# Sums z and dz off TensorE, mask by selects, and dWq blocks moved ahead of WK2, in a linear-attention block with its gradients

## The chip, the cores and the metric

The kernel runs on one core of one Trainium2 chip. The metric is device time in microseconds (us). The core has a TensorE (PE, matmuls), a VectorE (DVE), a ScalarE (ACT), a GpSimd (POOL) and a SyncE (SP, which mostly starts transfers). Every time below is the median of a kernel's executions, with the lowest and highest behind it. Ratios compare with executions of the kernel before on the same chip in the same session. A ratio is the mean time of one kernel's fast runs over the mean of the other's of the same rounds, so it is not quite the ratio of the medians quoted beside it. Its 95% interval stands in square brackets. A run counts as slow, and is left out of the ratio, when it is over 1.5% above the fastest of the same kernel.

## The reference, cut to what matters

The model is one block: a linear attention, then a gated MLP, each behind a layer norm, for 2048 tokens of width 640 (32 heads of 20). The program returns the output and the gradients of six of its inputs.

```python
def _A_ref(x, wqkv, wo):                     # H = 32, Dh = 20
    q, k, v = ...                            # x @ wqkv, split into heads
    phi = lambda t: jnp.where(t > 0, t + 1, jnp.exp(t)) + 1e-6
    pq, pk = phi(q), phi(k)
    kv  = jnp.einsum("bhsd,bhse->bhde", pk, v)
    z   = jnp.einsum("bhsd->bhd", pk)        # a sum over all tokens
    num = jnp.einsum("bhqd,bhde->bhqe", pq, kv)
    den = jnp.einsum("bhqd,bhd->bhq", pq, z)[..., None] + 1e-6
    return (num / den) ... @ wo
h   = x + _A_ref(_layernorm(x), wqkv, wo)
out = h + _B_ref(_layernorm(h), w_gate, w_up, w_down)
# returned: out and the vector-Jacobian product with grad_out
```

Two sums over the 2048 tokens (16 tiles of 128) matter here: z in the forward part, and dz, its gradient, in the backward part.

## The kernel before

TensorE makes both sums, as matmuls whose one operand is a block of ones (z) or the negative denominator terms nS (dz):

```python
# forward, behind the last projection
for ci, (n0, n1) in enumerate(NCH):          # two halves of 320 columns
    for t in range(ST):                      # 16 tiles of tokens
        nc.tensor.matmul(ps[q:q + H, ci, :320], lhsT=ones[:, :H], rhs=pk[:, t, n0:n1], ...)
...                                          # ScalarE and VectorE round z to two bf16 parts
def normalise(t):                            # VectorE, 4 tiles at a time, 4 times
    nc.vector.tensor_tensor(out=tz, in0=pq, in1=zb..., op=ALU.mult)          # needs z
    nc.vector.tensor_reduce(out=den[:], in_=hb4(tz), axis=AX.X, op=ALU.add)
    ...
    nc.vector.tensor_tensor(out=hb4(pq), in0=hb4(pq), in1=bc4(rall...), op=ALU.mult)
# pq is then transposed by SyncE's transfers, for the attention's output blocks ps_a
```

```python
# backward, stage of dhn and dp: one tile of 128 tokens at a time, the order of VectorE is the scheduler's
    pqr[u] = wk("pqr", pool=1)
    nc.gpsimd.dma_start(out=pqr[u][:], in_=scr_pq_v[:, u, :])        # GpSimd's queue
    nc.vector.tensor_tensor(out=hb(pqs_tm[:, u, :]), ...)            # phi(q), normalised: GT needs it
    ...
    # VectorE, "dp work" of tile u: pr, S1, nS1, pr, dp, pq, dp, dq
# after it: GT, then
dz_half(0); kv_blocks(dKVT, ...); dz_half(1)
...                                          # dz times E (one head's columns a row), x normalised
for i in range(DT): wk2(i)                   # WK2
...                                          # dzb: dz broadcast
dwqk(0, 0, 3)                                # three blocks of dWq, then the dK stage
```

The mask of the heads (ones in blocks) is made by two matmuls of E, a matrix built by GpSimd's selects.

The other names: xn is x normalised, Y its product with phi(k) summed over the tokens, KVT what Y becomes with the value weights, wvo the weights folded with KVT, ps_a the attention's output blocks. In the backward part dhn is the gradient behind the second layer norm (lb_ marks that norm's backward steps), cols its loaded operand, dp the gradient of the normalised phi(q), pqs_tm the normalised phi(q) itself, GT the product of dh and pqs_tm over the tokens. dWq is the gradient of the query weights, from dq and x normalised once more (hn); dKV and WK2 lead to dK. dwd is the gradient of w_down on its way out. A name with ps is a block in PSUM, where TensorE writes.

## Time and profile before

| | before |
|---|---|
| time, 3 runs | 821.57 us (821.45 to 823.08) |
| TensorE busy, at full clock | 813.3 of 820.0 us |
| first Y block / first ps_a / first dhn block start at | 57.2 / 100.1 / 456.0 us |
| last GT matmul / first dK matmul start at | 616.7 / 636.1 us |

The busy times, the chain at both places, and the slowed VectorE instructions stand in the prediction. Two further views matter later. The first gives, for stretches of time, the busy time of each engine, then the granted TensorE clock, the DMA share and the rate. It is the kernel before; the second line is the middle of the dhn stage.

```profile
core 0: us, PE busy (x) PEld busy (x) DVE busy (x) ACT busy (x) POOL busy (x), PEclk, DMA share, GB/s
87.50:106.00 18.50, 18.39 (x153) 11.39 (x151) 17.83 (x16) 9.32 (x12) 0.00 (x0) 1.00 0.58 136
517.00:578.00 61.00, 61.00 (x452) 43.94 (x450) 47.50 (x99) 17.48 (x28) 10.46 (x18) 1.00 0.69 189
```

VectorE is 54% busy on average, but 17.83 of 18.50 us just before and around the first ps_a block, where the normalising ends. In the dhn stage it has 13.5 of 61 us to spare.

### The profile page before, as it was taken

To read this page: it belongs to the slowest core of one execution; us is meant where nothing else is said; L and a number is where in the kernel's file an instruction comes from. 1 tells how busy PE (TensorE), PEld (TensorE's weight loads), DVE (VectorE), ACT (ScalarE), POOL (GpSimd) and SP (SyncE) were. 2 spreads that over 40 slices of the span, in tenths; PEclk is the share of its full clock that TensorE was granted. 3 is DMA by queue.
4 is the path that set the end of the run, shared out by engine and by line. 5 is a ranking of instruction groups with operands and counts; after the bars stand their busy time and mean duration, and the time that the engine had idled before them with its cause. 6 is when DMAs were issued, how large, how long until landed. Compare 5 with 4: busy or idle time off the path is not lost.

```text
span 820.0 us, 14053 instructions
## 1 busy us (share of the span) xinstructions
PE 813.3 (99%) x5540; PEld 521.0 (64%) x5540; DVE 442.9 (54%) x874; ACT 290.9 (35%) x412; POOL 187.6 (23%) x345
## 2 busy tenths in 40 slices
PE   8999999999999999999999999999999999999998
PEld 6776656555555555555566677777776777777675
DVE  6878776891087018810760147787884366631212
ACT  6982422770184126500741122322322133322010
POOL 3330022322412412221125311211210111112330
PEclk9999999999999999999999999999999999999999
DMA  9994589998769997894498757976498999899962
GB/s 297 186 343 113 140 174 281 307 204 176 191 126 209 203 224 160 185 245 115 106 237 171 256 139 217 222 205 166 116 216 171 170 167 187 167 198 272 222 176 76
DMA packets 278321, 158.61 MB, mean 193 GB/s; under 512 B 235052, under 2 KB 264877, under 8 KB 278256
## 3 DMA queue, kind: packets, MB, share of 16 engines
q1 hardware_dynamic: 251696, 82.12, 54.3%
q0 software_dynamic: 17744, 64.45, 25.8%
q10 hardware_dynamic: 8816, 11.16, 4.3%
q8 instruction: 43, 0.70, 0.4%
q14 instruction: 22, 0.18, 0.1%
HBM read 47.68 MB, written 53.66 MB: 124 GB/s over the span
## 4 chain that ended last, share of the span: by engine, by line
PE 82%; DVE 9%; ACT 3%; DMA 3%; issue 1%; SPq 1%; ACTq 0%; POOL 0%; DVEq 0%
PE ps_dw L627 21%; PE ps_dhn L109 14%; PE ps_dxn L877 8%; PE ps_o L937 7%; PE ps_dwqk L109 5%; PE pu L563 5%; PE pg L558 5%; PE ps_y L109 3%; PE ps_gt L678 3%; PE ps_dp L109 3%; PE ps_dk L109 3%; PE pdm L385 2%; DMA xr<-in_A_x_dram 2%; PE ps_dm L385 2%; DVE st L134 1%
## 5 line engine op out<-in xcount | busy, mean ns | idle before, releaser
L109 PE MATMUL ps_dhn<-wgT,cols 128*128 128x320 bf16 x864 | 119.5, 299 | 0.0
L627 PE MATMUL ps_dw<-dd,hn 128*128 128x448 bf16 (+1 forms) x640 | 118.8, 346 | 0.0
L109 PEld LDWEIGHTS <-cols 128*128 128x128 bf16 x864 | 84.5, 98 | 32.9
L627 PEld LDWEIGHTS <-hn 128*128 128x128 bf16 x640 | 62.6, 98 | 54.2
L629 DVE CAST dwev<-ps_dw 128x896 bf16<-128x896 f32 (+3 forms) x12 | 10.9, 907 | 122.9 <-PE ps_dw L627 122.9
L629 ACT CAST dwev<-ps_dw 128x896 bf16<-128x896 f32 (+1 forms) x20 | 17.6, 879 | 160.5 <-PE ps_dw L627 139.9
L592 POOL DMA_DIRECT2D scr_dT<-stg x64 | 34.7, 542 | 168.9 <-DMA stg<-dd 168.2
L147 DVE CUSTOM_DVE_ANT_0 lb_a<-lb_dy,hn 128x640 bf16<-128x640 bf16 x32 | 26.4, 825 | 75.4 <-ACT lb_dy L145 75.4
L563 PE MATMUL pu<-wgu,hnT 128*128 128x448 bf16 (+1 forms) x320 | 63.6, 346 | 0.0
L558 PE MATMUL pg<-wgu,hnT 128*128 128x448 bf16 (+1 forms) x320 | 63.6, 346 | 0.0
L937 PE MATMUL ps_o<-wd,mT 128*128 128x320 bf16 (+3 forms) x462 | 61.3, 295 | 0.0
L627 PE MATMUL ps_dw<-m_s,dh 128*128 128x448 bf16 (+1 forms) x320 | 60.5, 346 | 0.1
L877 PEld LDWEIGHTS <-ring 128*128 128x128 bf16 x480 | 47.0, 98 | 18.2
L937 PEld LDWEIGHTS <-mT 128*128 128x128 bf16 (+1 forms) x462 | 41.8, 97 | 17.6 <-issue 2.6
L877 PE MATMUL ps_dxn<-wqkvT,ring 128*128 128x320 bf16 x320 | 51.3, 299 | 0.0
L627 PEld LDWEIGHTS <-dh 128*128 128x128 bf16 x320 | 31.3, 98 | 27.4 <-issue 0.4
L563 PEld LDWEIGHTS <-hnT 128*128 128x128 bf16 x320 | 31.3, 98 | 27.1
L558 PEld LDWEIGHTS <-hnT 128*128 128x128 bf16 x320 | 31.3, 98 | 27.0
L298 PE MATMUL ps_kq<-wqk,xnT 128*128 128x320 bf16 x320 | 46.4, 299 | 1.0 <-ACT xnT L290 1.0
L385 PEld LDWEIGHTS <-dh2T 128*128 128x128 bf16 x320 | 31.1, 98 | 25.1 <-issue 0.2
L385 PE MATMUL ps_dm<-wdT,dh2T 128*128 128x448 bf16 (+1 forms) x240 | 46.9, 344 | 0.1
L145 ACT ACTIVATE lb_dy<-ps_dhn,rstd 128x640 bf16<-128x640 f32 x16 | 12.7, 793 | 85.5 <-PE ps_dhn L109 85.5
(162 smaller groups left out, 1277.1 us busy)
## 6 DMA issues: line engine op xcount, KB each, us to landing
scr_dT<-stg POOLq DMA_DIRECT2D x48, 224.0 KB, 3.3
cols<-scr_dT POOLq DMA_DIRECT2D x6, 1728.0 KB, 8.0
scr_m<-m_s POOLq DMA_DIRECT2D x12, 448.0 KB, 4.7
cols<-scr_dT ACTq DMA_DIRECT2D x2, 1728.0 KB, 9.5
out_dram<-dwev POOLq DMA_DIRECT2D x30, 112.0 KB, 3.4
scr_dT<-stg POOLq DMA_DIRECT2D x16, 192.0 KB, 2.6
scr_pk<-pk SPq DMA_DIRECT2D x4, 640.0 KB, 8.4
scr_pq<-pqa SPq DMA_DIRECT2D x4, 640.0 KB, 8.7
```

What stands on the lines that cost most here:

```text
L109: nc.tensor.matmul(ps[:, ci, :320], lhsT=lhs(k), rhs=rhs(k, *NCH[ci]), start=(start and k == 0), stop=(stop and k == n - 1))
L147: nc.vector.tensor_tensor_reduce(out=a[:], in0=dy[:], in1=xhat, scale=1.0, scalar=0.0, op0=ALU.mult, op1=ALU.add, accum_out=sums[:, 1:2])
L298: nc.tensor.matmul(ps[:, ci, :320], lhsT=xnT[:, t, k, :], rhs=wqk[:, k, w0 + n0:w0 + n1], start=(k == 0), stop=(k == DT - 1))
L385: nc.tensor.matmul(ps[:, c, :w], lhsT=dh2T[:, kt, (t + c) * P:(t + c + 1) * P], rhs=wdT[:, kt, o:o + w], start=(kt == 0), stop=(kt == DT - 1))
L558: nc.tensor.matmul(pg[:, c, :w], lhsT=hnT[:, kt, (t + c) * P:(t + c + 1) * P], rhs=wg[:, kt, 0:w], start=(kt == 0), stop=(kt == DT - 1))
L563: nc.tensor.matmul(pu[:, c, :w], lhsT=hnT[:, kt, (t + c) * P:(t + c + 1) * P], rhs=wg[:, kt, w:2 * w], start=(kt == 0), stop=(kt == DT - 1))
L592: nc.gpsimd.dma_start(out=scr_dT[t + c, :, KO[g]:KO[g] + GK[g], :], in_=stg[:, :GK[g], :])
L627: nc.tensor.matmul(ps[:, c, :w], lhsT=lhs(t), rhs=rhs(t), start=(t == 0), stop=(t == ST - 1))
L629: copy(out=ev[:, :len(parts), :w], in_=ps[:, :len(parts), :w])
L678: nc.tensor.matmul(ps[:, ci, :320], lhsT=dh1[:, t, i * P:(i + 1) * P], rhs=pqs_tm[:, t, n0:n1], start=(t == 0), stop=(t == ST - 1))
L877: nc.tensor.matmul(ps[:, ci, :320], lhsT=lhs[:, i, :], rhs=rhs[:, i, n0:n1], start=(k == 0 and i == 0), stop=(k == 2 and i == DT - 1))
L937: nc.tensor.matmul(po(t, ci), lhsT=mTs[t // 4][r, t % 4, j, :], rhs=wd[r, j, n0:n1], start=(t, ci) not in opened, stop=last)
```

## The change

Its intent is to take out of TensorE's stream all that others could do: z goes to GpSimd (6 tiles) and VectorE (10 tiles), dz to GpSimd, and the mask to GpSimd's selects. The waits between GT and dK are filled with dWq blocks, for which x is normalised earlier.

```diff
+    NZ = 6
+    def z_pool():                                   # GpSimd, behind its last power
+        zp = zf[:]                                  # 128 x 640, fp32
+        nc.gpsimd.tensor_tensor(out=zp, in0=pk[:, 0, :], in1=pk[:, 1, :], op=ALU.add)
+        for t in range(2, NZ):
+            nc.gpsimd.tensor_tensor(out=zp, in0=zp, in1=pk[:, t, :], op=ALU.add)
-        ps = mm("ps_z")                             # 32 matmuls, and the mask's 2
+        for n0, n1 in NCH:
+            zd = work.tile([P, 320], FP32, name="zd", tag="w")
+            nc.vector.tensor_reduce(out=zd[:], in_=pk[:, NZ:, n0:n1].rearrange("p t d -> p d t"), axis=AX.X, op=ALU.add)
+            nc.vector.tensor_tensor(out=zd[:], in0=zd[:], in1=zf[:, n0:n1], op=ALU.add)
+            ...                                     # rounded to two parts, zs and zl
         for i in range(DT):                         # Y blocks
-            if i == 0: mm_row(ps_z, ...)            # broadcast of z
+            if i == 1: mm_row(ps_zb, ...)
 ... the dhn stage, tile by tile
+        def dz_add(u):
+            for n0, n1 in NCH:
+                nc.gpsimd.tensor_tensor(out=hb(dst), in0=hb(pqs_tm[:, u, n0:n1]), in1=nS1[...], op=ALU.mult)
+                if u: nc.gpsimd.tensor_tensor(out=zf[:, n0:n1], in0=zf[:, n0:n1], in1=dst, op=ALU.add)
+            if u > 0: dz_add(u - 1)
 ... behind GT
-        dz_half(0); kv_blocks(dKVT, ...); dz_half(1)
-        ...                                         # E, x normalised
-        for i in range(DT): wk2(i)
-        dwqk(0, 0, 3)
+        ...                                         # x normalised
+        dwqk(0, 0)
+        kv_blocks(dKVT, ...)
+        dwqk(0, 1)
+        for i in range(3): wk2(i)
+        dwqk(0, 2)
+        for i in range(3, DT): wk2(i)
```

More of the change, by code (lines that the diff above doesn't have):

```diff
@@ L139, in ln_rstd @@
         eng.tensor_scalar(out=v[:, :nt], in0=mv[:, :nt, 1], scalar1=1e-5, scalar2=None, op0=ALU.add)
-        nc.gpsimd.tensor_tensor(out=rstd[:, t0:t0 + nt], in0=v[:, :nt], in1=nhalf[:, :nt], op=ALU.pow)
+        return nc.gpsimd.tensor_tensor(out=rstd[:, t0:t0 + nt], in0=v[:, :nt], in1=nhalf[:, :nt], op=ALU.pow)
     def ln_bwd(ps, xhat, rstd_col, resid, dst, pool):
@@ L233 @@
         nc.vector.memset(ones[:], 1.0)
-        E = const.tile([P, D], BF16, name="E")
-    ones32 = const.tile([P, P], BF16, name="ones32")
-    nc.vector.memset(ones32[:], 1.0 / H)
+        zf = const.tile([P, D], FP32, name="zf")
     zpad = const.tile([P, 4, 64], BF16, name="zpad")
@@ L253, with masks @@
     wo6 = wvo[:, 5:11]
+    def masks():
+        nc.gpsimd.memset(mask[:], 1.0)
+        for c0, n, p0 in ((0, 6, 0), (120, 2, 88)):
+            m = mask[:, c0:c0 + n * Dh]
+            for sign in (1, -1):
+                nc.gpsimd.affine_select(
+                    out=m, in_=m, pattern=[[-sign * Dh, n], [0, Dh]], compare_op=ALU.is_ge, fill=0.0,
+                    base=-p0 if sign > 0 else p0 + Dh - 1, channel_multiplier=sign)
     xn = big.tile([P, ST, D], BF16, name="xn", tag="B")
@@ L273, in ln1_rstd @@
     def ln1_rstd(t):
-        ln_rstd(mv1[:, t:t + 1, :], rstd1, t, 1)
+        return ln_rstd(mv1[:, t:t + 1, :], rstd1, t, 1)
     def ln1(t):
@@ L354 @@
                 ln1_stats(t + 2)
-                ln1_rstd(t + 2)
+                last_pow = ln1_rstd(t + 2).ins
             if t == 1:
@@ L363 @@
         kq_phi(ST - 1)
-        ps = mm("ps_z")
-        for ci, (n0, n1) in enumerate(NCH):
-            for t in range(ST):
-                q = t % 4 * H
-                nc.tensor.matmul(ps[q:q + H, ci, :320], lhsT=ones[:, :H], rhs=pk[:, t, n0:n1],
-                                 start=(t < 4), stop=(t >= ST - 4))
-        zs = [wk("zs"), wk("zl")]
-        nc.scalar.copy(out=half(zs[0][:]), in_=row(ps))
-        last_zs = nc.vector.tensor_tensor(out=half(zs[1][:]), in0=row(ps), in1=half(zs[0][:]), op=ALU.subtract).ins
-        ps_z = mm("ps_zb")
+    def z_pool():
[3 more added lines that the diff above has]
+            nc.gpsimd.tensor_tensor(out=zp, in0=zp, in1=pk[:, t, :], op=ALU.add)
+    with tc.manual_schedule(engines={EngineType.Pool}):
+        with tc.issue_after(last_pow):
+            z_pool()
+        masks()
     dm_t = {0: strips.tile([P, ST, GM], BF16, name="dm0", tag="S")}
@@ L408, in dm @@
             next(dms, None)
-    def masks():
-        tc.keep_in_program_order(nc.gpsimd.memset(E[:H, :], 1.0))
-        for sign in (1, -1):
-            tc.keep_in_program_order(nc.gpsimd.affine_select(
-                out=E[:H, :], in_=E[:H, :], pattern=[[sign, D]], compare_op=ALU.is_ge, fill=0.0,
-                base=0 if sign > 0 else Dh - 1, channel_multiplier=-sign * Dh))
-        for q in range(H, P, H):
-            nc.gpsimd.dma_start(out=E[q:q + H, :], in_=E[:H, :])
-        ps = mm("ps_mask")
-        pm = ps[:, 0, :160]
-        nc.tensor.matmul(pm[:, :120], lhsT=E[:H, 0:P], rhs=E[:H, 0:120], start=True, stop=True)
-        nc.tensor.matmul(pm[:, 120:], lhsT=E[:H, D - P:D], rhs=E[:H, 600:D], start=True, stop=True)
-        nc.scalar.copy(out=mask[:], in_=pm)
     pqsT = big.tile([P, DT, S], BF16, name="pqsT", tag="B")
@@ L459 @@
         KVT = yk[:, DT * D:].rearrange("p (j c) -> p j c", j=HG)
-        with tc.issue_after(last_zs):
-            nc.vector.memset(KVT, 0.0)
+        zs = [wk("zs"), wk("zl")]
+        for n0, n1 in NCH:
+            zd = work.tile([P, 320], FP32, name="zd", tag="w")
+            nc.vector.tensor_reduce(out=zd[:], in_=pk[:, NZ:, n0:n1].rearrange("p t d -> p d t"), axis=AX.X, op=ALU.add)
+            nc.vector.tensor_tensor(out=zd[:], in0=zd[:], in1=zf[:, n0:n1], op=ALU.add)
+            nc.vector.tensor_copy(out=zs[0][:, n0:n1], in_=zd[:])
+            nc.vector.tensor_tensor(out=zs[1][:, n0:n1], in0=zd[:], in1=zs[0][:, n0:n1], op=ALU.subtract)
+        nc.vector.memset(KVT, 0.0)
         for i in range(DT):
@@ L465 @@
             nc.scalar.copy(out=half(Yt[:, i, :]), in_=row(ps))
-            if i == 0:
-                mm_row(ps_z, lambda k: ones32[:], lambda k, n0, n1: zs[k][:, n0:n1], 2)
-                nc.scalar.copy(out=half(zb[:]), in_=row(ps_z))
-                masks()
             if 0 < i < 4:
                 dm(1)
+            if i == 1:
+                ps = mm("ps_zb")
+                mm_row(ps, lambda k: ones[:], lambda k, n0, n1: zs[k][:, n0:n1], 2)
+                nc.scalar.copy(out=half(zb[:]), in_=row(ps))
         dm(1)
@@ L679, in gt_part @@
                                      start=(t == 0), stop=(t == ST - 1))
+        def dz_add(u):
+            for n0, n1 in NCH:
+                dst = small.tile([P, 320], FP32, name="dzt", tag="stg", bufs=3, padded_shape=[P, 448])[:] if u else zf[:, n0:n1]
+                nc.gpsimd.tensor_tensor(out=hb(dst), in0=hb(pqs_tm[:, u, n0:n1]),
+                                        in1=nS1[:, u, n0 // Dh:n1 // Dh].unsqueeze(2).to_broadcast([P, 320 // Dh, Dh]),
+                                        op=ALU.mult)
+                if u:
+                    nc.gpsimd.tensor_tensor(out=zf[:, n0:n1], in0=zf[:, n0:n1], in1=dst, op=ALU.add)
         dq = [strips.tile([P, 8, D], BF16, name="dq", tag="S") for _ in range(2)]
@@ L717 @@
                     gt_part(gts[i], i, 0, ST - 3)
+            if u > 0:
+                dz_add(u - 1)
             pq = pqr.pop(u)
@@ L734 @@
             nc.vector.tensor_tensor(out=hb(dq[u // 8][:, u % 8, :]), in0=hb(dp[:]), in1=bc(rall[:, u, :]), op=ALU.mult)
+        dz_add(ST - 1)
     with tc.manual_schedule(engines={EngineType.SP, EngineType.DVE}):
@@ L776 @@
         Y = mat(2 * HG * P + HG * D, HG, D)
-        nc.gpsimd.dma_start(out=mat_v(scr_GT), in_=GT)
-        nc.vector.memset(dKVT, 0.0)
-        ps_dz = mm("ps_dz")
-        def dz_half(ci):
-            n0, n1 = NCH[ci]
-            for t in range(ST):
-                q = t % 4 * H
-                nc.tensor.matmul(ps_dz[q:q + H, ci, :320], lhsT=nS1[:, t, :], rhs=pqs_tm[:, t, n0:n1],
-                                 start=(t < 4), stop=(t >= ST - 4))
-        dz_half(0)
-        kv_blocks(dKVT, "ps_dkvt", lambda i, a, b: woT[:, i, a:b], lambda i, a, b: GT[:, i, a:b])
-        dz_half(1)
-        dzE = [wk("dzE"), wk("dzL")]
-        ps = ps_dz
-        nc.vector.tensor_tensor(out=half(dzE[0][:]), in0=row(ps), in1=half(E[:]), op=ALU.mult)
-        nc.vector.tensor_tensor(out=half(dzE[1][:]), in0=row(ps), in1=half(dzE[0][:]), op=ALU.subtract)
-        nc.vector.tensor_tensor(out=dzE[1][:], in0=dzE[1][:], in1=E[:], op=ALU.mult)
-        for t in range(ST):
-            nc.vector.tensor_scalar(out=xn_r[:, t, :], in0=xn_r[:, t, :], scalar1=mv1[:, t, 0:1],
-                                    scalar2=rstd1[:, t:t + 1], op0=ALU.subtract, op1=ALU.mult)
         wvk = strips.tile([P, 2, DT, D], BF16, name="wvk", tag="S")
@@ L802, with load_pqT @@
         WK2 = wvk[:, 1]
+        ring = strips.tile([P, 10, DT, P], BF16, name="ring", tag="S")
+        def load_pqT(v):
+            nc.sync.dma_start_transpose(out=ring[:, 4 + v % 3], in_=scr_pk[v * P:(v + 1) * P, :])
+            nc.sync.dma_start_transpose(out=ring[:, 7 + v % 3], in_=dq[v // 8][:, v % 8, :])
         def wk2(i):
@@ L808, in wk2, with dwqk @@
             nc.sync.dma_start_transpose(out=WV2[:, :, i * P:(i + 1) * P], in_=WK2[:, i, :])
-        for i in range(DT):
+        def dwqk(which, i):
+            ev = wk("dwqk", pool=i % 2)
+            ps = mm("ps_dwqk")
+            mm_row(ps, lambda t: xn_r[:, t, i * P:(i + 1) * P],
+                   lambda t, n0, n1: dq[t // 8][:, t % 8, n0:n1] if which == 0 else dk[:, t, n0:n1], ST)
+            nc.scalar.copy(out=half(ev[:]), in_=row(ps))
+            nc.gpsimd.dma_start(out=out_2[i * P:(i + 1) * P, which * D:(which + 1) * D], in_=ev[:])
@@ new lines @@
+        for v in range(3):
+            load_pqT(v)
+        nc.gpsimd.dma_start(out=mat_v(scr_GT), in_=GT)
+        nc.vector.memset(dKVT, 0.0)
+        for t in range(ST):
+            nc.vector.tensor_scalar(out=xn_r[:, t, :], in0=xn_r[:, t, :], scalar1=mv1[:, t, 0:1],
+                                    scalar2=rstd1[:, t:t + 1], op0=ALU.subtract, op1=ALU.mult)
+        dwqk(0, 0)
+        kv_blocks(dKVT, "ps_dkvt", lambda i, a, b: woT[:, i, a:b], lambda i, a, b: GT[:, i, a:b])
+        dzs = [wk("dzs"), wk("dzl")]
@@ L811 @@
+        nc.vector.tensor_copy(out=dzs[0][:], in_=zf[:])
+        nc.vector.tensor_tensor(out=dzs[1][:], in0=zf[:], in1=dzs[0][:], op=ALU.subtract)
+        dwqk(0, 1)
+        for i in range(3):
+            wk2(i)
+        dwqk(0, 2)
+        for i in range(3, DT):
             wk2(i)
         ps = mm("ps_dzb")
-        mm_row(ps, lambda k: ones[:], lambda k, n0, n1: dzE[k][:, n0:n1], 2)
+        mm_row(ps, lambda k: ones[:], lambda k, n0, n1: dzs[k][:, n0:n1], 2)
         nc.scalar.copy(out=half(dzb[:]), in_=row(ps))
-        def dwqk(which, i0=0, i1=DT):
-            for i in range(i0, i1):
-                ev = wk("dwqk", pool=i % 2)
-                ps = mm("ps_dwqk")
-                mm_row(ps, lambda t: xn_r[:, t, i * P:(i + 1) * P],
-                       lambda t, n0, n1: dq[t // 8][:, t % 8, n0:n1] if which == 0 else dk[:, t, n0:n1], ST)
-                nc.scalar.copy(out=half(ev[:]), in_=row(ps))
-                nc.gpsimd.dma_start(out=out_2[i * P:(i + 1) * P, which * D:(which + 1) * D], in_=ev[:])
@@ L825 @@
-        ring = strips.tile([P, 10, DT, P], BF16, name="ring", tag="S")
-        def load_pqT(v):
-            nc.sync.dma_start_transpose(out=ring[:, 4 + v % 3], in_=scr_pk[v * P:(v + 1) * P, :])
-            nc.sync.dma_start_transpose(out=ring[:, 7 + v % 3], in_=dq[v // 8][:, v % 8, :])
-        for v in range(3):
-            load_pqT(v)
-        dwqk(0, 0, 3)
         dk = big.tile([P, ST, D], BF16, name="dk", tag="B")
@@ L844 @@
             if t in (2, 3):
-                dwqk(0, t + 1, t + 2)
+                dwqk(0, t + 1)
             if t < ST:
@@ L870 @@
             if t >= ST:
-                dwqk(1, t - ST, t - ST + 1)
+                dwqk(1, t - ST)
             pkT, dqT, dkT = ring[:, 4 + u % 3], ring[:, 7 + u % 3], ring[:, u % 4]
@@ L890 @@
         nc.sync.dma_start(out=wd[64:, 13, :], in_=B_w_down[13 * P:F, :])
-        dwqk(1, LAG)
+        for i in range(LAG, DT):
+            dwqk(1, i)
         def dwo(j):
```

## The prediction

> **What bounds the kernel now.** I read the busy times first, then the chain of work that ended last, then the timelines around the two places where the sums z and dz are made, and last the groups of VectorE in the stage where dz would move to GpSimd.
>
> ```profile
> PE 813.3 (99%) x5540; PEld 521.0 (64%) x5540; DVE 442.9 (54%) x874; ACT 290.9 (35%) x412; POOL 187.6 (23%) x345
> ...
> PE 82%; DVE 9%; ACT 3%; DMA 3%; issue 1%; SPq 1%; ACTq 0%; POOL 0%; DVEq 0%
> ```
>
> TensorE is busy in 813.3 of 820.0 us at full clock. So this change can win only what it takes out of TensorE's stream, plus the small gaps at the same places; and it can lose whenever another engine makes TensorE wait. The chain (start, length, what) gives the pieces that the change touches:
>
> ```profile
> 56.45 0.84 PE ps_z L370 x17
> 57.29 4.45 PE ps_y L109 x32
> 61.74 0.54 PE ps_zb L109 x4
> 62.28 0.15 PE ps_mask L421
> 62.44 0.02 PE ps_mask L422
> ```
>
> ```profile
> 617.00 0.66 PE ps_dz L786 x16
> 617.66 1.54 PE ps_dkvt L484 x30
> 619.21 0.66 PE ps_dz L786 x16
> 619.86 0.43 PE ps_wk L128 x7
> 620.29 0.02 issue
> 620.31 1.30 ACT wvk L807 x2
> 621.61 0.04 issue
> 621.65 0.45 PE ps_wk L128 x7
> 622.10 0.64 PE ps_dzb L109 x4
> 622.75 13.52 PE ps_dwqk L109 x96
> ```
>
> The reader sees that z (32 matmuls) and dz (32) are already short, some 0.045 us a matmul, and that between 619.86 and 622.10 the chain leaves TensorE for ScalarE's evictions of WK2.
>
> The next lines decide how much is given back. They are from the timeline of all engines while phi(k), phi(q) of the last tokens are made, where GpSimd runs the two selects that build E:
>
> ```profile
> 50.41 1.49 POOL L414 TENSOR_SCALAR_AFFINE_SELECT E<-E 32x640 bf16<-32x640 bf16 x2
> 50.44 0.86 DVE L317 TENSOR_SCALAR phi_e<-phi_e 128x640 bf16<-128x640 bf16 x1
> ...
> 51.40 0.84 DVE L319 TENSOR_TENSOR pk<-phi_e,phi_r 128x640 bf16<-128x640 bf16 x1
> ...
> 52.16 0.31 DVE L317 TENSOR_SCALAR phi_e<-phi_e 128x640 bf16<-128x640 bf16 x1
> ...
> 52.58 0.49 DVE L319 TENSOR_TENSOR pqa<-phi_e,phi_r 128x640 bf16<-128x640 bf16 x1
> ```
>
> The same two VectorE instructions take 0.31 and 0.49 us when GpSimd is quiet and 0.86 and 0.84 us when a GpSimd select of 0.71 us runs beside them: 0.55 and 0.35 us longer, nearly what was left of the select at that moment.
>
> **What the Trainium skill says.** "SBUF — State Buffer", section "Who interferes with whom": VectorE and GpSimd share one pair of SBUF ports as an exclusive lock; a VectorE instruction with two SBUF inputs, or in a two-port mode, and a GpSimd instruction that reads SBUF shut each other out for a whole instruction; a reduction on VectorE does not contend. The trace agrees (0.86 against 0.31 us above). "GPSIMD Engine Reference", section "Elementwise — side-by-side cycle accounting": an add of two tensors costs GpSimd 4497 ns for 2048 elements a lane, some 2.6 cycles each. The trace has no wide GpSimd add; its selects with one input give 0.291 us for 128 and 0.708 us for 640 elements, so 0.19 us fixed and 0.81 ns an element. "VectorE: DVE Perf Modes", section "The perf-mode tier table": a reduction runs at one element a cycle. The trace agrees: 2560 elements in 2.82 us.
>
> **The change part by part.**
>
> Gains on TensorE. (1) z: its projections end at 55.55, the first Y block starts at 57.29. Without z the Y block can start at once, since the last pk tile is only its 16th operand: 1.74 us. (2) The mask matmuls: 0.17 us. (3) dz: 2 x 0.66 = 1.32 us. (4) WK2: five blocks of 7 matmuls; 21 of them took 1.06 us unhindered, so five take 1.77 us, against 622.10 - 619.86 = 2.24 us with the wait for evictions. Three and two, with a dWq block between, fit into the four PSUM buffers: 0.47 us. (5) dWq: 96 matmuls take 13.52 us; the 32 of a later block take 4.35, so three blocks need 13.04. The rest was TensorE pacing behind the normalising of x (16 x 0.36 us), which now starts before: 0.48 us. Sum 4.18 us, so the floor is 817.4 us. The dWq blocks themselves only move. The transposes that feed the last backward stage keep their number; load order changes, and WK2 is ready with room before the dxn blocks.
>
> Cost, z. VectorE reduces 10 of 16 tiles: 2 halves x 3200 elements at 2.82/2560 us is 3.5 us each, then an add, a cast and a subtraction of 320 columns, about 1.1 us: 9.2 us after the last phi at 57.6, so z is there at 66.8. The matmuls that broadcast it come after two Y blocks and one dm block: 55.55 + 4.35 + 4.35 + 1.89 = 66.15. TensorE would wait about 0.3 to 0.6 us; I take 0.3. The following normalisation starts 4 us later than now, but VectorE today waits 7.9 us for the KVT blocks, which covers that.
>
> GpSimd sums 6 tiles in 5 adds of 640 columns, right behind the last power at 49.76. From the select's rate and two reads an element an add is 0.19 + 640 x 2 x 0.81/1000 = 1.23 us; by the page's figure about 1.5 us. Estimates both. If each shuts VectorE out for its whole length less some 0.13 us (the 0.15 and 0.12 us by which the two cases above fall short), five add 5.5 us to VectorE. It had 0.2 us of idle time and 0.9 us of hindrance by the old selects there, so the xn tile of L270 at 55.12, which the Y block needs as its second operand, would come some 4.4 us late. Full effect on the start of Y: 4.4 us. I take 2.4 us, because VectorE's instructions come back to back there, may keep the ports, and GpSimd then does its adds in the free time later, up to 65 us.
>
> Cost, dz. Four GpSimd instructions of 320 columns a tile, 0.19 + 320 x 1.62/1000 = 0.71 us (0.88 by the page): 2.8 to 3.5 us a tile. VectorE's room there:
>
> ```profile
> 495.23 0.82 DVE L147 CUSTOM_DVE_ANT_0 lb_a<-lb_dy,hn 128x640 bf16<-128x640 bf16 x1 [1.67 <-ACT lb_dy L145]
> ...
> 496.86 0.82 DVE L727 TENSOR_REDUCE S<-pr 128x32 f32<-128x640 bf16 x1
> ```
>
> A tile takes 8.69 us of TensorE, and VectorE is idle in 1.7 of it. Shut out for 4 x (0.71 - 0.13) = 2.3 us, less one instruction (0.6 us) that falls beside the reduction, it loses 1.7 us a tile: just its idle time. At 0.88 us it is 2.3 us a tile, 0.6 us too much, and 15 tiles end 9 us late. The three tiles of lag hide that until the end, where GT, the normalising of x (611.9 + 5.8 = 617.7, needed in steps until 619.2) and the first dWq block then wait. I take 0.5 us. The dzb matmuls now come some 15 us after GT, so the last GpSimd sum is in time. GpSimd's own day, 3.2 us of work plus 1.6 us of DMA issue and waits in 8.69, leaves the column loads on time.
>
> Sum: 821.6 - 4.2 + 0.3 + 2.4 + 0.5 = 820.6 us.
>
> **The rivals.** A, the plain reading: GpSimd is idle there, its adds cost nothing. For it: 23% busy, 54% for VectorE, and someone chose 6 of 16 tiles so that z is just in time. Time 817.5 to 818.5. B, the port lock takes the place of the matmuls at the front: Y starts up to 3 us later than now, dz fits. Against A speaks the 0.86 us line. Time 821 to 823. C, as B, and VectorE becomes the bound of the stage of dhn and dp, because 7.0 us of its own and over 2 us of lock exceed 8.69 us: 826 to 835. For it: the page's GpSimd rate; against it: the room of three tiles, and that the lock falls partly on fixed overhead. D, GpSimd's loads behind dz_add come late (xnT_r waits now for the last dz): needed at 636, some 20 us after the queue is free; I see no cost.
>
> **Range and chances.** A gets about 0.4, B 0.35, C 0.2. The floor is 817.4, so faster by 2% (under 805.5) is all but excluded. Slower by 2% (over 838) needs C with GpSimd instructions of 1.1 us or more: 0.06. Eight in ten: 816.8 to 829.
>
> **What would show it.** In the changed profile: no group for z, dz and the mask on TensorE; TensorE's busy time some 3 us less; the first Y block starting at 55.6 (A), or at 58 to 60 (B) with phi and xn instructions of 1 to 1.8 us on VectorE beside GpSimd's adds; adds of 640 columns at 1.2 to 1.6 us and those of 320 at 0.7 to 0.9. In the dhn stage VectorE's two-input instructions get longer by some 2 us a tile and its waits for ScalarE's lb_dy shrink from 1.7 us; if that wait stays, C is wrong; if it is gone and GT or the first dWq block waits for VectorE, C is right. WK2 without a gap, and dWq blocks of 4.35 us. I would be wrong if GpSimd's adds leave VectorE's durations unchanged, or if they last over 2 us.

## The result, and the profile after

The changed kernel takes 846.04 us (841.93 to 849.68, 4 runs) against 822.33 (821.45 to 823.60, 4 runs) of the kernel before in the same session. The ratio is 1.0286 [1.0228, 1.0344]: slower, where the prediction gave that 0.06. The profiled execution, 849.68 us, is the slowest of the four; its numbers lean to the bad side.

From the page of the changed kernel, the busy times and the shares of the chain:

```profile
PE 820.0 (97%) x5474; PEld 524.1 (62%) x5474; DVE 493.2 (58%) x879; ACT 290.7 (34%) x410; POOL 252.5 (30%) x411
...
PE 77%; DVE 13%; DMA 6%; issue 2%; POOL 1%; SPq 1%; ACT 1%; DVEq 0%; POOLq 0%
```

TensorE runs 66 instructions less, as intended, and yet is busy 6.7 us longer, and the chain leaves it oftener. VectorE's busy time grew by 50 us, although z's reductions, additions and roundings are only 2 x (5.62 + 0.49 + 0.32 + 0.49) = 13.8 us of work. What TensorE waited for (total us, times, longest):

```profile
PE ps_gt L675 <- DVE pqs_tm L707: 7.0, 2, 4.7
PE ps_dhn L110 <- DMA cols<-scr_dT: 5.6, 1, 5.6
PE ps_y L110 <- DVE xn L278: 3.8, 2, 2.1
PE ps_a L110 <- DMA wvo<-wvo: 2.2, 2, 1.6
PE ps_zb L110 <- DVE zs L456: 1.6, 1, 1.6
```

Before, no wait of TensorE except those for the first tiles was above 0.3 us. The waits fall into two groups: the first Y block and what follows it, and the stage of dhn with GT. The first group in the timeline, GpSimd's sums beside VectorE:

```profile
49.33 0.49 DVE L327 TENSOR_TENSOR pqa<-phi_e,phi_r 128x640 bf16<-128x640 bf16 x1
49.38 1.69 POOL L375 TENSOR_TENSOR zf<-pk 128x640 f32<-128x640 bf16 x1
49.73 1.52 DVE L278 TENSOR_SCALAR xn<-x_tm,mv,rstd 128x640 bf16<-128x640 bf16 x1
...
51.15 5.95 POOL L377 TENSOR_TENSOR zf<-zf,pk 128x640 f32<-128x640 f32 x4
51.17 1.55 DVE L325 TENSOR_SCALAR phi_e<-phi_e 128x640 bf16<-128x640 bf16 x1
...
52.83 1.53 DVE L327 TENSOR_TENSOR pk<-phi_e,phi_r 128x640 bf16<-128x640 bf16 x1
```

Each of VectorE's instructions of 0.3 to 0.5 us waits one add through and ends soon after it; the lock is as the prediction has it. The same stretch by windows shows a term that the prediction lacks, in the column before the last two:

```profile
58.00:60.00 2.00, 0.35 (x1) 0.00 (x1) 1.79 (x6) 1.91 (x4) 0.83 (x3) 0.50 0.96 334
60.00:62.00 2.00, 1.91 (x8) 1.11 (x9) 1.86 (x4) 0.22 (x1) 0.00 (x0) 0.50 0.13 44
62.00:64.00 2.00, 2.00 (x9) 1.15 (x8) 2.00 (x1) 0.00 (x0) 0.00 (x0) 0.50 0.90 306
```

From 55.8 to 60.1 us TensorE did almost nothing (0.49 us of work). Its granted clock fell to 0.50 at 57.9, after 2.1 us of standing still, and came back at 64.7: 9 matmuls fit into 2 us there, against 17 in the 2 us from 66. The Trainium skill describes this in "TensorE: Matmul & The Clock Gate", section "What's actually happening": after an idle window of some 3.4 us the clock falls to half. I had not looked at that page. The half clock is in this trace (single matmuls of up to 474 ns, against 299), but not one length of idle time before it: 2.1 us here, 4.2 us at the wait for cols (idle from 582.7, half clock from 586.9). The profile has four such stretches, 23.9 us in all, in which TensorE was busy for some 19 us. If that work takes half the time at full clock, they cost some 9.5 us (an estimate). That is more than the matmuls taken away, and explains why TensorE is "busier" after the change.

Where the 28.0 us between the two profiles' spans (820.0 and 848.0) arose, by the start of the first matmul of each group:

| stretch | before | after | difference |
|---|---|---|---|
| start to first Y matmul | 57.2 | 57.9 | +0.7 |
| first Y matmul to first dhn matmul | 398.8 | 407.0 | +8.2 |
| first dhn matmul to last GT matmul | 160.7 | 182.2 | +21.5 |
| last GT matmul to first dK matmul | 19.4 | 16.7 | -2.7 |
| first dK matmul to the end | 183.9 | 184.2 | +0.3 |

The gain of 2.7 us is what was planned there: 2.27 us were predicted for dz, WK2 and the pacing of dWq. The five waits shown above (20.2 us) and the estimate for the half clock (9.5) make 29.7 us, near to the 28.0 us plus the 3 us of matmuls that TensorE no longer runs.

### The profile page after: what moved, and what is told of

Same layout as the page of the kernel before. It is cut to its first block, busy times and chain, and to the rows that moved or that the text cites. A ratio compares the mean times of both kernels' runs of the same rounds, so it can differ in the third digit from the quotient of the medians.

```text
span 848.0 us, 13992 instructions
## 1 busy us (share of the span) xinstructions
PE 820.0 (97%) x5474; PEld 524.1 (62%) x5474; DVE 493.2 (58%) x879; ACT 290.7 (34%) x410; POOL 252.5 (30%) x411
## 4 chain that ended last, share of the span: by engine, by line
PE 77%; DVE 13%; DMA 6%; issue 2%; POOL 1%; SPq 1%; ACT 1%; DVEq 0%; POOLq 0%
PE ps_dw L624 21%; PE ps_dxn L874 8%; PE ps_o L935 7%; PE pg L555 7%; PE pu L560 7%; PE ps_dhn L110 6%; PE ps_dwqk L110 5%; PE ps_dm L391 5%; DMA dwd<-scr_dwdT 3%; PE ps_dk L110 3%; PE ps_a L110 3%; PE pdm L391 2%; PE ps_y L110 2%; DVE st L135 1%; DVE zd L454 1%
## 5 line engine op out<-in xcount | busy, mean ns | idle before, releaser
L110 PE MATMUL ps_dhn<-wgT,cols 128*128 128x320 bf16 x864 | 122.1, 303 | 5.6 <-DMA cols<-scr_dT 5.6
L152 ACT ACTIVATE lb_a<-hn,lb_k 128x640 bf16<-128x640 bf16 x32 | 29.5, 921 | 49.5 <-DVE lb_k L151 35.3
```

The source lines that it names most:

```text
L110: nc.tensor.matmul(ps[:, ci, :320], lhsT=lhs(k), rhs=rhs(k, *NCH[ci]), start=(start and k == 0), stop=(stop and k == n - 1))
L152: nc.scalar.activation(out=a[:], in_=xhat, func=ACT.Identity, scale=k[:, 1:2], bias=k[:, 0:1])
```

## The experiments

Sixteen kernels ran, in four sessions. My first theory was the lock: GpSimd's sums hold the ports that VectorE needs, VectorE falls behind, and TensorE waits. The rivals were that the sums fill GpSimd's queue and make its loads late, that VectorE's own added work (the reductions) is the cost, and later, that only the order of VectorE's instructions changed.

### One half at a time

**Both sums back on TensorE**, with the selects, the early normalising of x and the new order kept:

```diff
-        with tc.issue_after(last_pow): z_pool()
+        ps = mm("ps_z"); ...                        # 32 matmuls as before
-            if u > 0: dz_add(u - 1)
+        ps_dz = mm("ps_dz"); ...                    # 32 matmuls behind GT, times E
```

> Both sums back on TensorE; the selects for the mask, the order of the dWq blocks and the early normalising of x stay. If the whole loss comes from the two sums: no TensorE wait over 1 us outside start and tail, clock 1.00 throughout, and 820 to 821 us, that is 0.95 us (WK2 0.47, dWq 0.48) plus 0.17 us (mask matmuls) below before. If the order of the dWq blocks or the late transposes carry part of the loss: above 823 us.

It took 822.13 us (821.87 to 823.84), ratio 1.0006 [0.9994, 1.0019]. The whole loss is in the two sums. The gain hoped for did not show: the first Y matmul started at 58.6 us here, against 57.2, and from there to the end the trace is 1.2 us shorter.

**Only z back on TensorE** (dz stays on GpSimd):

> z back on TensorE, dz left on GpSimd. Changed kernel: the first dhn matmul starts at 465 us against 456 before (9 us of the loss), and dhn to the end of GT takes 182 us against 161 (21 us). If the two losses are independent: dhn starts at 456 and the run takes about 21 - 2 us more than before, 838 to 843 us. If the late start feeds the second loss: less than 835 us.

833.46 us (832.98 to 834.71), ratio 1.0144 [1.0129, 1.0160].

**Only dz back on TensorE** (z stays on GpSimd and VectorE):

> dz back on TensorE, z left on GpSimd and VectorE. If independent: dhn starts at 465, dhn to the end of GT takes 161 us again, and the run takes about 9 - 1 us more than before, 828 to 831 us. If dz alone isn't what lengthens the dhn stage, that stage stays over 170 us.

831.96 us (831.38 to 834.82), ratio 1.0129 [1.0114, 1.0144].

So dz alone costs 1.44% and z alone 1.29%; their sum, 2.73%, is within the interval of the full change (1.0228 to 1.0344). By my criterion for the second run, under 835 would have meant that the late start feeds the second loss. The sum says otherwise: the halves add up. I had drawn the criterion from the one profiled execution, the slowest of four.

### What the lock holds

**GpSimd fills instead of sums**, of about the same length, in the full change; wrong:

```diff
-        nc.gpsimd.tensor_tensor(out=zp, in0=zp, in1=pk[:, t, :], op=ALU.add)
+        nc.gpsimd.memset(zp.bitcast(BF16), 1.0)     # and likewise in dz_add
```

> Wrong result on purpose: each GpSimd add and multiply of the two sums becomes a GpSimd fill of about the same length that reads nothing from SBUF (896 and 1280 two-byte elements, 0.8 and 1.1 us by the rate of the fills seen). GpSimd's queue stays as full. If the shared ports are the cause (theory L): VectorE's two-input instructions keep 0.49 and 0.82 us, dhn to the end of GT returns to 161 to 163 us, the first Y block starts before 57 us, and what is left is the late z of VectorE's reductions: 822 to 828 us in all. If GpSimd's full queue, which also issues the loads, is the cause (theory Q): the dhn stage stays at 175 us or more with the wait for the cols load.

851.89 us (849.29 to 853.67), ratio 1.0362, no better at all. My expectation fell, and the groups of VectorE in the dhn stage say why:

```profile
L730 DVE TENSOR_TENSOR pr<-dp,pqr 128x640 bf16<-128x640 bf16 x12 | 20.6, 1720 | 0.1
L151 DVE TENSOR_SCALAR lb_k<-lb_s 128x2 f32<-128x2 f32 x15 | 20.1, 1338 | 0.5
...
L153 DVE TENSOR_TENSOR lb_a<-lb_a,lb_dy 128x640 bf16<-128x640 bf16 x15 | 7.3, 489 | 4.1 <-ACT lb_a L152 4.0
L154 DVE TENSOR_TENSOR dh<-lb_a,dh 128x640 bf16<-128x640 bf16 x15 | 7.3, 484 | 0.1
```

The layer norm's instructions with two inputs (the last two lines) are as fast as in the kernel before (483 and 484 ns), as "SBUF — State Buffer", section "Who interferes with whom", has it for a GpSimd that only writes. But an instruction on 128x2 elements with one input takes 1338 ns on average, against 219. One of them took 5.96 us, through three transfer issues on GpSimd and four fills of 0.86 to 1.18 us. Of the instructions with two inputs only pr is longer (1720 ns, against 492): at the four places that were read in the timeline it starts just behind such an instruction and ends with it. The longest is another instruction with one input, near the end of the stage:

```profile
606.00 16.12 DVE L737 TENSOR_SCALAR pqr<-pqr 128x640 bf16<-128x640 bf16 x1
```

It lasted through fifteen fills and two transfer issues. The dh of the last tile stands behind it, and TensorE waited 17.0 us for dh1T, which is made from dh. A fill is no neutral stand-in for a sum.

**Powers instead of sums** for dz, on the kernel with z on TensorE; six powers of 128x1 a tile touch almost no memory; wrong:

```diff
-                nc.gpsimd.tensor_tensor(out=hb(dst), ..., op=ALU.mult)
-                if u: nc.gpsimd.tensor_tensor(out=zf[:, n0:n1], ..., op=ALU.add)
+                for k in range(3):
+                    nc.gpsimd.tensor_tensor(out=zf[:, n0 + k:n0 + k + 1], in0=rstd2[:, u:u + 1], in1=nhalf[:, :1], op=ALU.pow)
```

> Wrong result on purpose. z on TensorE; the four GpSimd instructions of dz a tile become six powers of 128x1, about 0.65 us each and so about as long (3.9 us a tile), which read and write one column. The powers seen in the first stage do not lengthen VectorE's instructions. Theory L (the SBUF ports): VectorE undisturbed, dhn to the end of GT 161 us as before instead of 174, time 821 to 823 us. Theory Q (GpSimd's queue too full to issue its loads in time): the stage stays at 170 us or more, time over 830 us.

823.24 us (821.93 to 824.32), ratio 1.0007 [0.9991, 1.0022]. The windows of 61 us in the middle of the dhn stage are the sharpest comparison. First with the dz sums, then with the powers, engines in the order PE, PEld, DVE, ACT, POOL:

```profile
518.00:579.00 61.00, 61.00 (x451) 43.93 (x449) 59.80 (x96) 17.49 (x28) 36.65 (x48) 1.00 0.84 199
```

```profile
519.00:580.00 61.00, 61.00 (x451) 43.94 (x450) 47.27 (x99) 17.48 (x28) 37.48 (x63) 1.00 0.66 197
```

GpSimd is as busy in both (36.65 and 37.48 us). VectorE does the same work; it takes 59.80 us beside the sums and 47.27 beside the powers, and 47.50 in the kernel before. A tile takes 8.69 us, so the lock costs VectorE 12.3 / 7.02 = 1.75 us a tile, of the 1.9 us that were idle. VectorE has 1.2 of 61 us left, and TensorE does not wait yet. GpSimd being busy is not the cause; what it touches is.

**dz for every second tile only** (the result passes the tolerance though half of dz is missing):

```diff
-            if u > 0:
+            if u > 0 and u % 2 == 1:
                 dz_add(u - 1)
```

> Wrong result on purpose. z on TensorE; dz on GpSimd for every second tile only. Theory L with VectorE's idle time of 1.7 us a tile as the threshold: a tile with dz costs VectorE about 2.4 us, so over two tiles 2.4 us against 3.4 us of idle time: no lag, dhn to the end of GT 161 to 163 us, time 821 to 824 us. If the loss is proportional to the number of GpSimd instructions, with no threshold: half of the 13 us, 827 to 829 us.

828.24 us median, but 824.01, 827.44 and 829.03 in the fast runs and 838.67 in one that counts as slow; ratio 1.0056 [1.0032, 1.0080]. In the profiled, fastest one TensorE waits 3.1 us for the last pqs_tm. With half the sums VectorE has room on average, and the time depends on how the last tiles fall. The ratio lies between the two theories and settles neither.

### The front: lock, stride, or neither

**The reductions of z with adjacent elements**, on the kernel with dz on TensorE; z is wrong on purpose, but passes the tolerance:

```diff
-  in_=pk[:, NZ:, n0:n1].rearrange("p t d -> p d t")                        # step of 640 elements
+  in_=pk[:, NZ:, n0:n1].rearrange("p t (a b) -> p t a b", b=10)            # adjacent
```

> Wrong result on purpose. dz on TensorE, z on GpSimd and VectorE as in the run that took 832.0 us; but VectorE's two reductions of 3200 elements read along the row (groups of 10 neighbours) and not with a step of 640 elements. If the step is what makes one reduction take 5.6 us and not the 3.5 us of the prediction: 3.5 us each, z ready 4.2 us earlier, TensorE's waits for z gone, and the first dhn matmul at 461 to 463 us instead of 466. If the length comes from something else: 5.6 us again and no change.

830.65 us (829.71 to 831.16), ratio 1.0101 [1.0087, 1.0115]. The reductions, first with the step and then without it (min/median/max in ns):

```profile
L464 DVE TENSOR_REDUCE zd<-pk x2: 5611/5615/5619, 62.2 to 69.5; 128x320 f32<-128x3200 bf16 x2
```

```profile
L464 DVE TENSOR_REDUCE zd<-pk x2: 3479/3482/3486, 62.3 to 67.5; 128x320 f32<-128x3200 bf16 x2
```

The prediction's 3.5 us is right for adjacent elements, from which its rate came; the change steps over 640 elements, and pays 1.61 times as much. TensorE's wait for zs is gone, but the first dhn matmul comes at 464.7 us, later than the 461 to 463 expected.

**No GpSimd sums of z** (one fill and ten powers in their place, the reductions as in the change), then **the same with adjacent elements**; z wrong in both:

```diff
-        nc.gpsimd.tensor_tensor(out=zp, in0=pk[:, 0, :], in1=pk[:, 1, :], op=ALU.add)   # and four more
+        nc.gpsimd.memset(zp, 1.0)
+        for k in range(10):
+            nc.gpsimd.tensor_tensor(out=zf[:, k:k + 1], in0=rstd1[:, ST - 1:ST], in1=nhalf[:, :1], op=ALU.pow)
```

> Base: the changed kernel with dz back on TensorE (831.96 us alone, ratio 1.0129). Here the five GpSimd adds of z are replaced by one fill and ten powers of 128x1, so nothing that shares memory ports with VectorE runs on GpSimd while x is normalised and the last feature maps are made; VectorE's two reductions, its additions and its roundings stay. z is wrong on purpose. Port theory of the front (the adds stretch VectorE's instructions from 0.3-0.5 to 1.5 us, which stops TensorE in the first Y and halves its clock): the first Y has no wait for xn (4.0 us before) and no matmul at half clock, and the time falls by 4 to 7 us to 825-828 (ratio about 1.0045-1.008). Chain theory (the two reductions of 5.6 us and what follows them on VectorE set the stage's end, whatever the adds do): the wait for xn goes, but the wait for zs and the late ps_a grow by as much, and the time stays above 830.

> As the run before, and the two reductions of VectorE read adjacent elements (3.48 us each as measured, 5.61 with a step of 640). z is wrong on purpose. If lock and slow reductions are the two parts of z's loss and add up: 822-825 (ratio 1.001-1.004), since 2 us more are saved than in the run before. If a third part exists (the reductions' mere presence on VectorE between the last feature map and the normalisation, some 10 us), it stays above 826.

826.36 us (826.08 to 828.24), ratio 1.0050 [1.0021, 1.0079], and 824.22 us (822.15 to 825.78), ratio 1.0018 [0.9988, 1.0048]. The waits of TensorE: the kernel with z's lock and step, then without the lock, then without both.

```profile
PE ps_y L110 <- DVE xn L279: 4.0, 2, 2.1
PE ps_a L110 <- DMA wvo<-wvo: 2.4, 2, 1.7
PE ps_zb L110 <- DVE zs L466: 2.2, 1, 2.2
```

```profile
PE ps_zb L110 <- DVE zs L466: 3.8, 1, 3.8
...
PE ps_a L110 <- DMA wvo<-wvo: 0.5, 1, 0.5
```

```profile
PE ps_a L110 <- DMA wvo<-wvo: 3.4, 2, 1.9
```

Without the lock the wait for xn is gone, and part of it comes back as a wait for zs, the end of the slow reductions. Without both, TensorE still waits 3.4 us before the attention's blocks. The order of these four traces, by the start of the first dhn matmul (456.0 in the kernel before):

| | lock | no lock |
|---|---|---|
| step of 640 | 466.4 | 461.7 |
| adjacent | 464.7 | 457.5 |

The lock is worth 4.7 or 7.2 us, the step 1.7 or 4.2, together 8.9; these are single executions, and the last is the fastest of its four. By the ratios of all runs the lock is worth 0.79 or 0.83% and the step 0.28 or 0.32%.

In the best corner nothing is gained, although TensorE has no z matmuls and starts its Y blocks at 55.7 us. It is through the last block ahead of ps_a at 98.9 us, against 100.3 in the kernel before, so most of the 1.74 us was still there. Then it waits for the transposes of wvo, as the last view says, and the first ps_a matmul comes at 100.3 us, against 100.1. VectorE's normalising is not late: its third part starts at 87.9 us, against 89.3. SyncE's transposes of wvo last from 92.2 to 101.8 us, against 92.5 to 99.5. In its queue they stand behind transfers that came some 5 us later than before (the transposes of pqsT at 84.9, against 79.9). That this slows them is not shown; why they were late stays open, and with it whether the 1.74 us could be had.

### The stage of dhn: loads and order

**cols from ScalarE's queue**, in the full change. In the profile of the changed kernel GpSimd's queue stood 8.61 us at a wait for dwd, and the load of cols behind it came late:

```profile
574.84 0.55 POOL L711 DMA_DIRECT2D out_dram<-dwd  x1 [8.61 <-DMA dwd<-scr_dwdT]
...
580.16 0.75 POOL L162 DMA_DIRECT2D cols<-scr_dT  x1
...
588.35 2.05 PE L110 MATMUL ps_dhn<-wgT,cols 128*128 128x320 bf16 x7 [5.61 <-DMA cols<-scr_dT]
```

```diff
-                    load_cols(t // 2 + 1)
+                    load_cols(t // 2 + 1, act_load)
```

> The changed kernel in full, with only the loads of cols issued from ScalarE's queue instead of GpSimd's, where they stood behind a wait of 8.6 us for dwd. If TensorE's wait of 5.6 us for cols (and the half clock after it, some 2 us more) is a loss of its own: 838-841 against 846. If it is only where a lag of VectorE shows first (the same lag would be waited for at GT): 844-848, with the wait for pqs_tm at GT grown from 7.0 to 10 us or more.

844.62 us (842.32 to 846.70), ratio 1.0276 [1.0241, 1.0310]. The wait for cols is gone from its profile, the wait for pqs_tm at GT is 7.6 us, neither smaller nor the 10 us of the second theory. The times do not separate it from the full change. Late cols may be part of why the profiled execution was the slowest of four; how often they come late in others stays open.

**Order.** The built programs show that VectorE's order differs in the last three tiles. Before, and in the run with powers, the three last pqs_tm (which GT needs) stand together. With dz_add, the scheduler puts the next to last behind a whole tile of dp work and the last behind another, since their loads stand behind the sums in GpSimd's queue. In time, the last three pqs_tm start at 597.0, 598.2 and 600.0 in the kernel before. With dz on GpSimd:

```profile
595.44 1.46 DVE L153 TENSOR_TENSOR lb_a<-lb_a,lb_dy 128x640 bf16<-128x640 bf16 x1
596.82 1.40 DVE L732 SCALAR_TENSOR_TENSOR nS<-S,rall 128x32 bf16<-128x32 f32 x1
...
605.06 0.82 DVE L703 TENSOR_TENSOR pqs_tm<-pqr,rall 128x640 bf16<-128x640 bf16 x1
...
611.51 1.47 DVE L703 TENSOR_TENSOR pqs_tm<-pqr,rall 128x640 bf16<-128x640 bf16 x1
...
619.91 0.81 DVE L703 TENSOR_TENSOR pqs_tm<-pqr,rall 128x640 bf16<-128x640 bf16 x1
```

So the run with powers had changed two things, the lock and the order. Four runs take them apart. **pqr loaded from ScalarE's queue**, on the kernel with z on TensorE: the lock stays, the order is again the one of before:

```diff
-                nc.gpsimd.dma_start(out=pqr[u][:], in_=scr_pq_v[:, u, :])
+                act_load(pqr[u][:], scr_pq_v[:, u, :])
```

> Base: z back on TensorE, dz on GpSimd (833.46 us, ratio 1.0144). Only the loads of pqr (phi(q), one tile each) are issued from ScalarE's queue instead of GpSimd's, where they stand behind the dz sums; with that, VectorE's built order in the last three tiles is again the one of the kernel before. All GpSimd sums and their lock stay. If the order is the main cause: 821 to 826 (ratio below 1.005), the wait for pqs_tm at GT 0 to 2 us instead of 8.4. If the lock is the cause by itself: 830 or more, with that wait at 6 us or more.

831.70 us (830.58 to 831.84), ratio 1.0108 [1.0091, 1.0125], against 1.0144 with the loads in GpSimd's queue. GT no longer waits. Its last matmul starts at 617.8, and yet the first dK matmul only at 645.7: the wait has moved one block on.

```profile
PE ps_dwqk L110 <- DVE hn L811: 7.0, 6, 1.9
```

```profile
618.00:622.00 4.00, 0.81 (x4) 0.19 (x2) 4.00 (x8) 0.69 (x1) 2.52 (x4) 0.99 1.25 128
622.00:626.00 4.00, 0.91 (x3) 0.23 (x3) 4.00 (x7) 0.00 (x0) 3.98 (x6) 0.50 0.92 189
626.00:630.00 4.00, 3.31 (x10) 0.96 (x10) 4.00 (x11) 0.00 (x0) 0.92 (x2) 0.50 1.15 325
```

The change has put a dWq block directly behind GT; it needs x normalised (hn) and every tile of dq. VectorE, busy without a gap, starts its last dq at 625.9 us, against 611.1 in the kernel before. TensorE's single matmuls then also run at half clock. **The order of the change without any sums**, on a kernel with nothing changed but the order behind GT (below):

```diff
-                nc.vector.tensor_tensor(out=hb(pqs_tm[:, u, :]), ...)       # the last two
+            last_dq = nc.vector.tensor_tensor(out=hb(dq...), ...)
+            with tc.issue_after(last_dq.ins):
+                nc.vector.tensor_tensor(out=hb(pqs_tm[:, u + 1, :]), ...)
```

> Base: the kernel with only the dWq order changed (821.17). Nothing runs on GpSimd for dz; only the last two normalisations of phi(q) are put behind the dp work of the tile before, the order that the changed kernel has. Before, pqs_tm of the last tile comes at 600.0; here two tiles of dp work of 4.4 us each stand ahead of it, so about 607 to 609. If the order alone costs: 823 to 827 with a wait for pqs_tm at GT of 2 us or more. If the order costs only together with a VectorE that is already late: 821 to 822.5 and no such wait (the run with powers had its last one at 606.6 without one).

823.75 us (822.22 to 829.33), ratio 1.0027 [0.9989, 1.0065], with a wait of 1.1 us at GT: between the two expectations, and not clear of noise. (The profiled execution is the one of 829.33; it also has a wait of 3.8 us in a later stage, which I cannot tie to the edit.) **The order mended in part, the loads left where they are**:

```diff
+            if u in (ST - 3, ST - 2):
+                with tc.issue_after(pqs_ins[u + 1]):
                     nc.vector.tensor_tensor(out=pr[:], in0=dp[:], in1=pq[:], op=ALU.mult)
```

> Base: z back on TensorE, dz on GpSimd (833.46 us). The loads stay in GpSimd's queue; only the dp work of each of the last two tiles but one is held behind the next tile's normalisation of phi(q). If order is the main cause: 822 to 828 (one of the two positions is regained, and the loads still come late). If the lock is: 830 or more.

834.18 us (832.65 to 836.94), ratio 1.0145: no gain, the wait at GT is one of 6.3 us. **pqr from ScalarE's queue in the full change**:

> The changed kernel in full (846.04 us, ratio 1.0286), with only the loads of pqr issued from ScalarE's queue. z's loss of some 10 us stays. If the order is the main cause of dz's 12 us: 831 to 837 (ratio 1.011 to 1.018), and the wait for pqs_tm at GT below 2 us. If the lock is: 841 or more.

843.64 us (842.83 to 844.48), ratio 1.0253 [1.0233, 1.0273]; the wait for pqs_tm is gone and one of 7.0 us for hn has come, as in the smaller kernel. The order theory asked for 837 or less and falls. The late loads, with the order that they bring, are worth about a third of a per cent in both pairs (1.0144 and 1.0108, 1.0286 and 1.0253); in the second the intervals overlap. The late VectorE is the rest.

### Is there something to keep?

**Both sums on TensorE, and the selects held until z is done**, so that they cannot delay the first powers:

> As the run with both sums on TensorE, which was no faster than before (822.1 against 821.9 us): there the scheduler had moved the mask selects ahead of the first powers on GpSimd (0.44 us in the start), and its new order from GT to dK took 1.2 us less than before. Here the selects wait until VectorE has made the low part of z. If that account is right, the start is as before, the phi instructions on VectorE no longer take 0.84 to 0.86 us beside a select, and the time is 820 to 821 us, 1 to 2 us under before. If the order of the dWq blocks gains nothing: 821.5 us or more.

821.89 us (821.04 to 823.25), ratio 0.9998 [0.9985, 1.0010]: by its expectation (821.5 or more) no gain, although the first Y matmul starts at 57.6 us and GT and dK are 18.0 us apart.

**Only the order behind GT** (dWq blocks between dKV and WK2, x normalised ahead); z, dz and mask as before:

```diff
+        dwqk(0, 0)
         kv_blocks(dKVT, ...)
+        dwqk(0, 1)
         for i in range(3): wk2(i)
+        dwqk(0, 2)
         for i in range(3, DT): wk2(i)
-        dwqk(0, 0, 3)
```

> The kernel before with nothing changed but the order between GT and the dK stage: dWq blocks set between dKV and WK2, x normalised ahead of them; z, dz and the mask stay on TensorE. The prediction puts 0.47 + 0.48 us on this: 821.0 to 821.3 against 822.0 of the kernel before, ratio 0.9985 to 0.9995. If the two runs with both sums on TensorE (ratios 1.0006 and 0.9998) lost this gain in the mask's selects, it shows here; if the gain is given back later (in the dK stage), the ratio is 1.0000 here too.

821.17 us (820.87 to 822.99) against 822.13, ratio 0.9988 [0.9964, 1.0011]. In its trace the last GT matmul and the first dK matmul are 18.4 us apart, against 19.4: the predicted 0.95 us. The time agrees in its median, but the interval includes 1, so a faster kernel is likely and not shown.

## Why the prediction was wrong

The mechanism of the lock was right and named: GpSimd's sums and VectorE shut each other out. Rival C, that VectorE becomes the bound of the dhn stage, is nearest to what happened, though VectorE just kept up in the middle of that stage and became the bound in its last four tiles. It was given 826 to 835 us and a chance of 0.2, and the total lies above even that. By the steps:

- **The cost of dz, "I take 0.5 us", failed.** The term measured 1.44% (12 us) net of dz's own gain. The steps ahead of it were good: the lock takes 1.75 us a tile from VectorE (1.7 predicted), and the sums last 0.74 us (the product) and 0.99 us (the add) in the median, against 0.71 to 0.88 estimated for each. The lag was also hidden until the end, as predicted: with z on TensorE the twelfth of the sixteen dq starts 2.6 us late, counted from the start of the stage. What failed is the size of that end. The last four tiles bring the lag to 16.2 us (13.8 with the loads elsewhere). VectorE has no idle time with which to catch up, GpSimd works off its backlog beside it (seven sums between 595.0 and 603.9 us), and from one dq to the next it takes 13.2 us there instead of 8.7. GT waits 8.4 us (or, with the loads elsewhere, the first dWq block 7.0 us), and the half clock adds its share. That I had written "GT, the normalising of x ... and the first dWq block then wait" and then put 0.5 on it was a choice against my own argument.
- **The cost of z failed in three terms.** For the lock the prediction worked out a "full effect" of 4.4 us on the xn tile that starts at 55.1, and then took 2.4, since GpSimd might do its adds later, in free time. The adds ran back to back from 49.4 to 57.1 us, and that tile came at 59.6: 4.5 us late, the full effect. (By the prediction's own working the page's figure gives 1.6 us for such an add, not 1.5; four took 1.40 in the median, the first 1.69.) The reductions took 5.61 us and not 3.5, since the rate came from adjacent elements, and TensorE waited 1.8 us for zs and zl, with 0.3 predicted. The wait of 2.2 us for the transposes of wvo is not in the sum at all. "VectorE today waits 7.9 us for the KVT blocks, which covers that" held: VectorE still waits 1.9 us for them in the changed kernel.
- **The half clock was missing** from the sum. In all falls in the kept traces TensorE had worked at most 1.4 of the 3.4 us before, and half clock then lasted 3.4 or 6.8 us, in three cases longer. In the first Y block waits of 3.8 us were followed by 5.0 us of work at half clock, so they cost some 6.3 us (an estimate).
- **The gain for z, 1.74 us, did not show** even with the lock and the slow reductions gone: TensorE was 1.4 us ahead at its last block before ps_a and then waited for wvo.
- **The gains behind GT were right**: 2.7 us measured between GT and dK (2.27 predicted), 1.0 for the order alone (0.95 predicted). WK2 had no gap and the dWq blocks their full rate.
- **Rival D, "I see no cost", was too quick.** Loads in GpSimd's queue did come late, cols by way of dwd and pqr by way of dz_add. The second is worth about 0.36% (1.0144 less 1.0108, from two sessions); the first could not be separated in the times.

Some 66 matmuls of 0.045 us were taken from the engine that bounds the kernel, 3 us in all, and two engines that share ports were set to do it in some 80 us of work (GpSimd 65 us more busy, VectorE's 13.8).

## What to carry to other kernels

An engine at 54% on average may have little room where you need it (here 1.1 of 7.7 us ahead of the first Y block, 1.9 of 8.7 us a tile in the dhn stage): read its busy time in the stretch where the work will lie, and what the work behind it leads to. Before moving work to GpSimd, add what it will take from VectorE's instructions beside it; if that uses up VectorE's idle time, expect a lag where VectorE's work comes without gaps (here the last four tiles), and nothing to make up for it. Where a wait leaves TensorE idle for some microseconds, add the work behind it that may run at half clock. And test with a stand-in that keeps the engine busy but leaves the memory alone, then check that the stand-in has not changed the order of anything else.

## What the Trainium skill lacked or had wrong

- "SBUF — State Buffer", section "Who interferes with whom", says that the loser is blocked for the whole instruction. With back-to-back work on GpSimd it was blocked for several instructions: one of 128x2 elements took 5.96 us, while GpSimd issued three transfers and ran four fills of 0.86 and 1.18 us, and one of 128x640 took 16.12 us, through fifteen fills. That two-input instructions do not contend with a GpSimd that only writes was confirmed where they did not stand behind a blocked one (489 and 484 ns).
- "VectorE: DVE Perf Modes", section "The perf-mode tier table", gives a reduction one rate. With a step of 640 bf16 elements 3200 elements took 5.61 us, and 3.48 us adjacent: a factor of 1.61. The page nearest to it, "Vector Engine (DVE) Microarchitecture Reference", section "Measured stream behaviour on trn2", measures a 32-bit source that hops at every element; none has a factor for a reduction of bf16.
- "TensorE: Matmul & The Clock Gate", section "What's actually happening", speaks of idle windows and does not say how little work makes one. TensorE fell to 0.50 after 2.1 us without work (57.9 us in the changed kernel), and also where single matmuls came in between: in a stretch of 8 us with 1.7 us of work and no wait above 1.9 us.
- "GPSIMD Engine Reference", section "Elementwise — side-by-side cycle accounting", holds: its 4497 ns for 2048 elements give 1.41 us for 640 columns (an estimate), and four of the five adds took 1.40 in the median. It has one row for two-input operations, in fp32; the add of two bf16 inputs took 1.69 us, and for 320 columns products of bf16 inputs took from 0.71 us and fp32 adds from 0.85 us.
